# A recurrence and an MLP on one core: the seven-product form for one more token group, and two score buffers in every unit

## The chip, the cores and the metric

The kernel runs on one core of a Trainium2 chip. A core has TensorE (PE, matrix products), VectorE (DVE), ScalarE (ACT), GpSimd (POOL) and SyncE (SP), each with a queue of its own that it works off in order, and DMA engines that all of them can start. The metric is the device time of one execution in microseconds, as the median over several runs.

## The reference

A gated linear recurrence with complex decays over 768 steps for 4 x 8 heads of width 48, and behind it an MLP with squared ReLU over all 3072 tokens, all of it in float32:

```python
mag = np.sqrt(a_re * a_re + a_im * a_im)
scale = np.minimum(mag, 0.999) / (mag + 1e-06)
a_re_n, a_im_n = (a_re * scale, a_im * scale)
for t in range(S):
    ar, ai = (a_re_n[:, :, t, :, None], a_im_n[:, :, t, :, None])
    new_re = ar * S_re - ai * S_im
    new_im = ar * S_im + ai * S_re
    kv = np.einsum('bhd,bhe->bhde', k[:, :, t], v[:, :, t])
    S_re, S_im = (new_re + kv, new_im)
    y[:, :, t] = np.einsum('bhd,bhde->bhe', q[:, :, t], S_re)
x = y.transpose(0, 2, 1, 3).reshape(3072, 384)
h = x @ w_in            # 384 x 2048
out = np.maximum(h, 0.0) ** 2 @ w_out   # 2048 x 384
```

## The kernel before

**Units.** The 3072 tokens are cut into six units of 512. For each unit the kernel does a *chain*, then *pairs*, then *dense*. The chain (VectorE and ScalarE above all) makes the decays' running products and from them two scaled arrays, Q~ and K~. `pairs` takes the heads in four pairs: Q~ and K~ are turned (the tokens into the columns) into a buffer `QT`; TensorE makes the scores of two heads (`sc`), VectorE multiplies them by a causal mask into a buffer `A`, and a mix of A with the values v and of Q~ with the running state gives the outputs (`yp`), which are copied and moved by DMA into `xT`. In all units but the first, the turning is four transposes on VectorE, copies on ScalarE and nine DMAs, eight of them from SyncE's queue. `dense` is the MLP, in two groups of 256 tokens: a hidden layer of 48 matmuls of 256 columns into three PSUM blocks d0 to d2, ReLU and square on ScalarE into `g`, and a second layer.

**The second layer in three forms.** The plain form (the end of `dense`) multiplies each of the two 128-token halves by all 16 blocks of w_out: 2 x 16 matmuls of 384 columns. `eight` cuts tokens, hidden width and output width in two each and makes eight products. `seven` does the same with seven products, by sums and differences of operands: each product is two calls of `half` with four matmuls of 192 columns, so 56 matmuls. It needs sums of quarters of w_out, made once by `sums_of_w2` on VectorE (eight instructions, which also overwrite a quarter of w_out in place, so that the plain form can't be used afterwards), sums of quarters of g for each group (`put`, eight on VectorE), and seven additions of 128x192 into the output tiles (`add`).

**Who uses which.** Groups are named (unit, group). The list `SEVEN` has the groups in the seven-product form: both groups of the units 1 to 5. Unit 0 has the plain form in both.

**Shared space.** A tile `T` of 4608 columns has three thirds. While the weights are brought in it stages raw pieces of them; in unit 1 it is a third QT buffer, a third A buffer and the second value buffer `vv[1]`; from `sums_of_w2` on it holds the three sums of quarters of w_out. `ROOM` is the number of units, counted from the first, that use this: `vs(n)` gives the value buffer, and unit 1 has three QT and three A buffers, where all others have two.

**What sets the order.** The program is a list of steps with their reads and writes. A planner (`Plan.order`) puts them into a sequence for each engine: of the steps that are ready at the time, the one with the lowest number in the table `ORDER` goes first. Where it counts on a longer stop of TensorE it puts in small matmuls of the identity (`idle`). The sequence is fixed when the kernel is built; on the chip an instruction starts when all ahead of it in its engine's queue have, and its data are there.

**Lines.** L1850 is the hidden layer's matmul, L1897 the plain second layer's, L2051 a `half` of the seven-product form, L2065 a `put`, L2074 an `add`, L2036 the sums of w_out, L1679 a transpose of `turn` and L1691 its DMAs, L1732 the scores, L1738 the mask, L1762 the new state (`keep`), L1777 its sums on VectorE, L1790 and L1794 the mix, L880 the identity matmuls, L1076 the loads of decays, Q and K, and L1091 those of v. L1143, L1153, L1214, L1228, L1243, L1247, L1248, L1265, L1270 and L1277 are the chain's products on VectorE.

Of the kernel before, what the change touches and what calls it, by code (L numbers as in the profile page):

```python
# [767 lines left out]
def fast_path(ctx, tc, q, k, v, a_re, a_im, moe_w_in, moe_w_out, out, flag, ots, blocks_of):  # L768
# [1073 lines left out]
    def dense(n, grp):  # L1842
# [43 lines left out]
        if n >= FAST:  # L1886
            (seven if joint else eight)(n, grp)
            return
# [380 lines left out]
```

## Time and profile before

| | us |
|---|---|
| median of three runs | 650.94 (650.93 to 651.6) |
| the profiled execution | 652.71 |
| its span | 651.0 |
| granted TensorE clock in it, mean | 0.997 |
| first dense matmul of unit 0 | 84.84 |
| first scores of unit 1 | 151.20 |
| first dense matmul of unit 1 | 186.28 |
| first dense matmul of unit 2 | 283.50 |

The profile is of one execution. It gives every instruction's start and length by engine, what ended the idle time before it, and the landing of DMAs; times within it are from the span's start. A float32 matmul leaves two records, and the recorded lengths of neighbours overlap, so that the pace of TensorE is read from the length of a row of matmuls and not from the mean of one. Lines are those of the kernel before; in the kernel after, lines behind the table are one higher, and two less than that between the removed and the added call of `sums_of_w2`.

### The profile page before, as it was taken

Reading aid. Unit: us, or ns where it says so; the run is one execution under the profiler, and the core shown is the slowest. Engines: PE = TensorE matmul, PEld = TensorE weight load, DVE = VectorE, ACT = ScalarE, POOL = GpSimd, SP = SyncE. Lnnn points to the kernel's source line nnn. Section 1 sums busy time; section 2 is a strip of 40 time slices with the busy share of each in tenths; the row PEclk is TensorE's granted clock in tenths of the full one; section 3 lists DMA queues with packets and bytes.
Section 4 is the critical chain, followed back from the end, with each engine's and each line's share of the span. In section 5 each row is a group of like instructions: output and inputs, shape, how many; then the busy total and the mean of one; then the engine's idle time right before and its main releaser. Section 6 shows DMA issues by size and latency. Waiting matters only on the chain.

```text
span 651.0 us, 13374 instructions
## 1 busy us (share of the span) xinstructions
PE 641.1 (98%) x5046; PEld 575.9 (88%) x5046; DVE 571.2 (88%) x1187; ACT 382.8 (59%) x652; POOL 152.4 (23%) x258
## 2 busy tenths in 40 slices
PE   8998999999999999999999999999999999999998
PEld 7988987578778988999988998989999989988997
DVE  7999999999799998988997996995979998359993
ACT  7989889956665265368166648156658164145500
POOL 6503455123200022051043051121050030022210
PEclk9998999999999999999999999999999999999999
DMA  7972679237620156352176354165260162257651
GB/s 224 298 255 57 163 213 203 72 89 189 165 82 2 37 126 149 93 143 52 49 161 146 73 131 88 24 152 159 58 171 16 45 143 66 61 202 242 209 184 31
DMA packets 34630, 81.79 MB, mean 126 GB/s; under 512 B 7894, under 2 KB 13411, under 8 KB 34556
## 3 DMA queue, kind: packets, MB, share of 16 engines
q0 software_dynamic: 17024, 58.60, 33.6%
q1 hardware_dynamic: 15356, 20.04, 12.1%
q10 hardware_dynamic: 2176, 2.20, 1.2%
q8 instruction: 42, 0.69, 0.5%
q14 instruction: 32, 0.26, 0.1%
HBM read 48.76 MB, written 4.72 MB: 82 GB/s over the span
## 4 chain that ended last, share of the span: by engine, by line
PE 73%; DVE 12%; ACT 4%; DMA 3%; issue 2%; SPq 0%; POOL 0%; DVEq 0%; ACTq 0%; POOLq 0%
PE d L1850 24%; PE d L2051 24%; PE d L1897 5%; PE sc L1732 5%; PE yp L1790 3%; PE tr L1762 2%; PE d L1943 2%; PE yp L1794 2%; PE tr L1943 2%; DVE f L1243 1%; PE sc L1943 1%; DMA aq<-in_a_im_dram 1%; PE d L1710 1%; DVE g L2065 1%; DVE aq L1228 1%
## 5 line engine op out<-in xcount | busy, mean ns | idle before, releaser
L1850 PE MATMUL d<-xT,w 128*128 128x256 f32 x912 | 203.2, 380 | 0.0
L1850 PEld LDWEIGHTS d<-xT,w 128*128 128x128 f32 x912 | 171.8, 190 | 24.0 <-issue 0.4
L2051 PE MATMUL d<-w,g 128*128 128x192 f32 x576 | 101.0, 327 | 0.0
L2051 PEld LDWEIGHTS d<-w,g 128*128 128x128 f32 x576 | 94.3, 190 | 1.2 <-issue 0.4
L1882 ACT ACTIVATE g<-d 128x512 f32<-128x512 f32 x76 | 45.0, 592 | 81.7 <-PE d L1850 79.0
L2051 PE MATMUL d<-T,g 128*128 128x192 f32 x432 | 77.1, 329 | 0.4 <-DVE g L2065 0.3
L2051 PEld LDWEIGHTS d<-T,g 128*128 128x128 f32 x432 | 70.6, 190 | 2.0 <-DVE g L2065 0.6
L2007 POOL DMA_DIRECT2D out_dram<-ot x22 | 12.5, 569 | 202.3 <-DVE ot L2074 181.3
L1682 ACT COPY QT<-aq 32x512 f32<-32x512 f32 x57 | 35.0, 615 | 39.7 <-DVE aq L1679 27.9
L1639 POOL DMA_DIRECT2D KC<-f x56 | 35.0, 630 | 80.8 <-DVE f L1593 30.3
L2065 DVE TENSOR_TENSOR g<-g 128x512 f32<-128x512 f32 x72 | 48.1, 685 | 4.8 <-PE d L2051 4.0
L1883 ACT ACTIVATE g<-g 128x512 f32<-128x512 f32 x80 | 50.5, 631 | 2.6
L1679 DVE STREAM_TRANSPOSE aq<-f 128x768 f32<-128x768 f32 x40 | 49.0, 1277 | 0.3
L1800 ACT COPY yt<-yp 112x512 f32<-112x512 f32 x24 | 26.5, 1106 | 34.2 <-PE yp L1794 34.2
L880 PEld LDWEIGHTS d<-ident 128*128 128x128 f32 x348 | 42.6, 203 | 3.0 <-POOL ident masks.py:199 1.7
L880 PE MATMUL d<-ident 128*128 128x128 f32 x348 | 43.3, 287 | 1.7 <-POOL ident masks.py:199 1.7
L1593 DVE TENSOR_TENSOR f<-aq 128x768 f32<-128x768 f32 (+1 forms) x56 | 44.0, 838 | 0.5
L1897 PE MATMUL d<-w,g 128*128 128x384 f32 x128 | 43.7, 491 | 0.0
L1732 PE MATMUL sc<-QT 96*64 96x128 f32 (+1 forms) x736 | 41.0, 258 | 1.5 <-ACT QT L1713 0.8
L1732 PEld LDWEIGHTS sc<-QT 96*64 96x64 f32 x736 | 37.1, 140 | 4.6 <-issue 2.3
L1738 DVE TENSOR_TENSOR A<-sc,mask 128x512 f32<-128x512 f32 x45 | 29.8, 681 | 9.2 <-PE sc L1732 9.2
L1897 PEld LDWEIGHTS d<-w,g 128*128 128x128 f32 x128 | 23.7, 190 | 15.0 <-issue 0.4
(276 smaller groups left out, 1167.5 us busy)
## 6 DMA issues: line engine op xcount, KB each, us to landing
QT<-aq SPq DMA_DIRECT2D x152, 64.0 KB
f<-in_moe_w_in_dram POOLq DMA_DIRECT2D x8, 768.0 KB, 6.0
f<-in_moe_w_out_dram POOLq DMA_DIRECT2D x8, 768.0 KB, 5.0
out_dram<-ot POOLq DMA_DIRECT2D x22, 192.0 KB, 2.8
KC<-f POOLq DMA_DIRECT2D x20, 192.0 KB, 4.5
xT<-yt SPq DMA_DIRECT2D x36, 96.0 KB
aq<-in_q_dram POOLq DMA_DIRECT2D x8, 384.0 KB, 5.4
aq<-in_k_dram POOLq DMA_DIRECT2D x8, 384.0 KB, 5.7
```

What stands on the lines that cost most here:

```text
L880: plan = Plan(lambda b: pe.matmul(bank[b][:, 0:C], lhsT=ident, rhs=ident, start=True, stop=True), ["d2", "d1", "d0"], lambda ap: tc.nc.val ...
L1593: lambda j=j, r=r, o=o: dve.tensor_tensor(out=o[:, :, :, r * D:(r + 1) * D], in0=qk[:, j], in1=a[:, r], op=ALU.mult), late[z])
L1639: lambda i=i, queue=queue, lo=lo, hi=hi, a0=a0, a1=a1: queue.dma_start(out=kc[lo:hi, i], in_=nat[a0:a1]),
L1679: lambda nat=nat, dst=dst, j=j: dve.transpose(out=dst[:, j], in_=nat), rank)
L1682: lambda b=b, t=t, T6=T6: act.copy(out=t[32 * b:32 * b + 32, b], in_=T6[32 * b:32 * b + 32, i % 2, b]),
L1732: pe.matmul(sa[r:r + C // 2, j, :, lo:32], lhsT=T[:, j, 1, h, ts(late, C // 2)], rhs=T[:, j, 0, h].rearrange("p (c t) -> p c t", c=W)[:, : ...
L1850: pe.matmul(ps, lhsT=w1[:, f // FP, m, ts(f % FP, C)], rhs=xT[:, n % 2, m, ts(grp, G)], start=(m == 0), stop=(m == NM - 1))
L1882: act.activation(out=o, in_=ps, func=AF.Relu)
L1883: act.activation(out=o, in_=o, func=AF.Square)
L1897: pe.matmul(ps, lhsT=gt[:, f % 2, ts(i, C)], rhs=w2[:, f], start=(f == 0), stop=(f == NF - 1))
L2051: pe.matmul(bank[b][:, 0:DH], lhsT=gs(r, h)[:, j - 4 * h], rhs=w(j), start=first and j == 0, stop=last and j == NT - 1)
L2065: step("DVE", tt(4 * C), gk(x0, h) + gk(x1, h), gk(o, h), lambda: dve.tensor_tensor(out=gs(o, h), in0=gs(x0, h), in1=gs(x1, h), op=op), (0 ...
```

## The change

1. `SEVEN` is now all groups but the very first, so (0,1), the second group of the first unit, takes the seven-product form too. Its hidden layer is made in the pairs of blocks that this form needs (`fs`).
2. `sums_of_w2` is called behind the dense step of (0,0) instead of behind the pairs of unit 1. As it overwrites part of w_out, it must come behind the last plain product, which is now one group earlier, and its results go into the tile T.
3. T is then no longer free in unit 1, so `ROOM` goes from 2 to 1: unit 1 has two buffers of Q~ and of scores, as all others, and its values go into the first value buffer, in which unit 0 had its own.
4. The table `ORDER` has other numbers throughout.

```diff
-    ROOM = max(FAST, 2)
-    SEVEN = [(n, grp) for n in range(FAST, NU) for grp in range(2)]
+    ROOM = 1
+    SEVEN = [(n, grp) for n in range(NU) for grp in range(2)][FAST:]
...
-        fs = [(j, j + NT) if n >= FAST else (2 * j, 2 * j + 1) for j in range(NT)]
+        fs = [(j, j + NT) if joint else (2 * j, 2 * j + 1) for j in range(NT)]
...
-        if n >= FAST:
-            (seven if joint else eight)(n, grp)
+        if joint:
+            seven(n, grp)
             return
...
-        if n == FAST:
-            sums_of_w2()
...
                 dense(n, grp)
+            if (n, grp + 1) == SEVEN[0]:
+                sums_of_w2()
```

How the instructions stand now, at three places. The first is TensorE's queue ahead of the first scores of unit 1 (w1 and w2 are w_in and w_out, g the hidden layer, sc the scores, KC the gathered K~). Before:

```order
L1897 MATMUL d2_66<-w2_75,g_100 128x384 x2
L1850 MATMUL d1_65<-xT_99,w1_74 128x256 x6
L1850 MATMUL d2_66<-xT_99,w1_74 128x256 x6
L1850 MATMUL d1_65<-xT_99,w1_74 128x256 x6
L1850 MATMUL d0_64<-xT_99,w1_74 128x256 x6
L1897 MATMUL d1_65<-w2_75,g_100 128x384 x8
L1850 MATMUL d0_64<-xT_99,w1_74 128x256 x6
L1850 MATMUL d2_66<-xT_99,w1_74 128x256 x6
L1732 MATMUL sc1_114<-QT1_82 64x128 x8
```

After:

```order
L1898 MATMUL d2_66<-w2_75,g_100 128x384 x6
L1851 MATMUL d0_64<-xT_99,w1_74 128x256 x6
L1851 MATMUL d2_66<-xT_99,w1_74 128x256 x6
L1851 MATMUL d0_64<-xT_99,w1_74 128x256 x6
L1851 MATMUL d2_66<-xT_99,w1_74 128x256 x6
L1851 MATMUL d1_65<-xT_99,w1_74 128x256 x3
L881 MATMUL d0_64<-ident_101 128x128 x3
L1851 MATMUL d2_66<-xT_99,w1_74 128x256 x6
L1851 MATMUL d1_65<-xT_99,w1_74 128x256 x6
L1763 MATMUL tr1_116<-v0_85,KC0_83 64x48
```

The eight output matmuls of the second group that stood there are gone, and three identity matmuls stand there (two more stand earlier, ahead of the turning of the chain's totals). From the first dense matmul of unit 0 up to here the queue has 90 hidden-layer matmuls in both, and 40 output matmuls before against 32 now; the half products of the second group all stand behind this point.

The second place is VectorE's queue in the pairs of unit 1, up to its last two masks (St and S are the running state, g the operand sums' tile, f and aq the chain of unit 2). Before:

```order
L1738 TENSOR_TENSOR A0_93<-sc0_113,mask_103 128x512
L1265 SCALAR_TENSOR_TENSOR f0_78<-f0_78 128x4x144
L1228 TENSOR_TENSOR aq0_76<-aq0_76,f0_78 128x1536
L1270 TENSOR_TENSOR f0_78<-f0_78 128x4x48
L1243 TENSOR_TENSOR f0_78<-aq0_76 128x768 x2
L2036 TENSOR_TENSOR w2_75<-w2_75 128x4x192
L1777 TENSOR_TENSOR St1_96<-tr0_115,S1_92 96x96
L1777 TENSOR_TENSOR S0_91<-tr0_115,St1_96 96x96
L1143 TENSOR_TENSOR f1_79<-f1_79 128x768
L1738 TENSOR_TENSOR A0_93<-sc1_114,mask_103 128x512
L1738 TENSOR_TENSOR T_80<-sc0_113,mask_103 128x512
```

After:

```order
L2075 TENSOR_TENSOR ot0_62<-ot1_63,d2_66 128x192
L1374 TENSOR_REDUCE sums_104<-xn_90 128x1
L1154 SCALAR_TENSOR_TENSOR f0_78<-f0_78 128x768
L1158 SCALAR_TENSOR_TENSOR f0_78<-f0_78 128x768
L1144 TENSOR_TENSOR f1_79<-f1_79 128x768
L1215 SCALAR_TENSOR_TENSOR f0_78<-f0_78 128x768
L1229 TENSOR_TENSOR aq0_76<-aq0_76,f0_78 128x1536
L1244 TENSOR_TENSOR f0_78<-aq0_76 128x768 x2
L1778 TENSOR_TENSOR St1_96<-tr0_115,S1_92 96x96
L1778 TENSOR_TENSOR S0_91<-tr0_115,St1_96 96x96
L1739 TENSOR_TENSOR A0_93<-sc0_113,mask_103 128x512
L1739 TENSOR_TENSOR A1_94<-sc1_114,mask_103 128x512
```

Counted from the program's start to the last mask of unit 1, VectorE's queue has eight more operand sums (L2065), six more sums of w_out (L2036) and two more additions (L2074), and one L1265 and one L1270 fewer. Before the first mask of unit 1 the two queues hold the same work but for one L1373, and before the first transpose of unit 1 but for one L1277, which now stand behind.

The third place is SyncE's queue in the same pairs (yt are the outputs on their way to xT). Before:

```order
L1691 DMA QT1_82<-aq0_76 32x512 x8
L1691 DMA T_80<-aq0_76 32x512 x8
L1691 DMA QT0_81<-aq1_77 32x512 x8
L1691 DMA QT1_82<-aq1_77 32x512 x6
L1808 DMA xT_99<-yt0_97 48x512
```

After:

```order
L1692 DMA QT0_81<-aq0_76 32x512 x8
L1692 DMA QT1_82<-aq0_76 32x512 x8
L1692 DMA QT0_81<-aq1_77 32x512 x8
L1809 DMA xT_99<-yt0_97 48x512 x2
L1692 DMA QT1_82<-aq1_77 32x512 x8
```

The third pair's copies go into the first pair's buffer now, so they have to wait until the first pair's mix has read it, and the fourth pair's for the second pair's mix.

261 rows, old and new, of the table ORDER are left out of this document.

## The prediction

> **What bounds the kernel now.** First the page: busy shares, then the forty slices.
>
> ```profile
> span 651.0 us, 13374 instructions
> PE 641.1 (98%) x5046; PEld 575.9 (88%) x5046; DVE 571.2 (88%) x1187; ACT 382.8 (59%) x652; POOL 152.4 (23%) x258
> ...
> PE   8998999999999999999999999999999999999998
> DVE  7999999999799998988997996995979998359993
> ```
>
> TensorE is busy in every slice, so whatever leaves its queue should shorten the run. But VectorE is at 9 too, from the second slice to about the thirteenth (16 us each), and only later falls to 5 to 8. The change lies in that first part, so the share alone doesn't say which engine sets the pace there. I therefore cut the part into three stages at events of TensorE (the view of windows; columns: length, busy time and instructions of PE, weight loads, DVE, ACT, POOL, granted clock, DMA share, GB/s).
>
> ```profile
> 85.00:151.20 66.20, 66.20 (x273) 50.20 (x273) 64.52 (x132) 54.74 (x90) 23.70 (x36) 1.00 0.60 142
> 151.20:186.28 35.08, 34.72 (x397) 26.14 (x397) 29.75 (x45) 25.22 (x41) 9.02 (x13) 1.00 0.67 177
> 186.28:283.50 97.22, 96.65 (x781) 89.10 (x780) 90.32 (x185) 50.35 (x87) 10.79 (x18) 1.00 0.29 76
> ```
>
> Stage A (85.0 to 151.2) is the first unit's dense work on TensorE, beside the second unit's chain on VectorE; both are full. Stage B (151.2 to 186.28) is the second unit's head pairs, with what is left of the first unit's dense work as filler. Stage C is the second unit's dense work up to the third unit's. Why does B begin at 151.2? The timeline, rows of four engines:
>
> ```profile
> 139.60 3.28 DVE L1679 STREAM_TRANSPOSE aq<-f 128x768 f32<-128x768 f32 x3
> 142.23 6.42 SPq L1691 DMA_DIRECT2D QT<-aq  x8
> 151.01 0.77 POOL L1076 DMA_DIRECT2D aq<-in_a_im_dram  x1 [8.51 <-DMA T<-aq]
> 151.20 1.09 PE L1732 MATMUL sc<-QT 96*64 96x128 f32 x16
> ```
>
> VectorE turns the first pair, SyncE issues eight copies of it until 148.65, and GpSimd, whose next load overwrites their source, is let go at 151.01. The first scores follow at 151.20. So B starts when VectorE's data arrive, and TensorE's queue ahead of it happened to be just long enough. That is the row on which my forecast turns.
>
> **The change, part by part.**
>
> *Products.* In the chain of waits:
>
> ```profile
> 111.66 9.03 PE d L1897 x28
> ...
> 613.69 26.00 PE d L2051 x160
> ```
>
> One matmul is two records. A 384-column one takes 2 x 9.03/28 = 0.645 us, a 192-column one 2 x 26.00/160 = 0.325 us. The old group has 32 of the first, 20.6 us; the new one 14 half products of 4, 56 of the second, 18.2 us. TensorE saves 2.4 us. ScalarE has one narrow copy for two wide ones and is busy 25.22 of 35.08 us in B: nothing.
>
> *Stage A.* The order ahead of the second unit's first scores keeps 90 hidden-layer matmuls but loses 8 of the group's 32 output matmuls, 8 x 0.645 = 5.2 us (the new products all stand behind those scores). The scores cannot come 5.2 us sooner: VectorE's queue ahead of the first pair's transposes is the same but for one L1277, which costs about 0.7 us. So B starts near 150.5, and TensorE idles for about 4.5 us in A, partly under the five identity matmuls now put there.
>
> *Stage B, TensorE alone.* It is busy 34.72 us. Out go 24 output matmuls (15.5 us), in come the 18.2 us: 37.4 us. From 150.5 that ends at 187.9 instead of 186.28. So with no further wait the saving has already become a loss of 1.6 us.
>
> *Stage B, VectorE.* It gets eight operand sums (L2065), most of the weight sums (L2036; they used to lie partly in C) and adds (L2074):
>
> ```profile
> L2065 DVE TENSOR_TENSOR g<-g 128x512 f32<-128x512 f32 x72 | 48.1, 685 | 4.8 <-PE d L2051 4.0
> L2074 DVE TENSOR_TENSOR ot<-ot,d 128x192 f32<-128x192 f32 x70 | 23.8, 349 | 13.8 <-PE d L2051 9.8 <-issue 3.5
> L1265 DVE SCALAR_TENSOR_TENSOR f<-f 128x576 f32<-128x576 f32 x12 | 8.9, 750 | 0.9 <-ACT f L1222 0.9
> L1270 DVE TENSOR_TENSOR f<-f 128x192 f32<-128x192 f32 x24 | 8.1, 352 | 0.3
> L2036 DVE TENSOR_TENSOR T<-w 128x768 f32<-128x768 f32 x4 | 3.8, 952 | 0.1
> ```
>
> In a row such instructions start sooner than their durations say:
>
> ```profile
> 179.14 0.68 DVE L1738 TENSOR_TENSOR A<-sc,mask 128x512 f32<-128x512 f32 x1
> 179.74 0.68 DVE L1738 TENSOR_TENSOR T<-sc,mask 128x512 f32<-128x512 f32 x1
> ...
> 196.97 0.96 DVE L2036 TENSOR_TENSOR T<-w 128x768 f32<-128x768 f32 x1
> 197.84 0.95 DVE L2036 TENSOR_TENSOR T<-w,T 128x768 f32<-128x768 f32 x1
> ```
>
> That is 0.60 and 0.87 us, 0.08 less than they last. Up to the last mask of the second unit, VectorE's queue gains 8 x 0.60, 6 x 0.87 and 2 x 0.26, and loses one L1265 (0.67) and one L1270 (0.27): 9.6 us more. Against this stand its waits in B before that mask:
>
> ```profile
> 161.62 0.69 DVE L1738 TENSOR_TENSOR T<-sc,mask 128x512 f32<-128x512 f32 x1 [1.17 <-PE sc L1732]
> 162.57 0.25 DVE L1777 TENSOR_TENSOR St<-tr,S 96x96 f32<-96x96 f32 x1 [0.26 <-ACT St L1770]
> 165.16 0.96 DVE L1153 SCALAR_TENSOR_TENSOR f<-f 128x768 f32<-128x768 f32 x1 [1.50 <-ACT f L1150]
> 168.81 0.69 DVE L1738 TENSOR_TENSOR A<-sc,mask 128x512 f32<-128x512 f32 x1 [0.83 <-PE sc L1732]
> 177.94 0.25 DVE L1777 TENSOR_TENSOR St<-tr,S 96x96 f32<-96x96 f32 x1 [1.43 <-ACT St L1770]
> ```
>
> 5.2 us that more work can fill. The last mask ended at 179.74 + 0.68 = 180.4, so it now ends at 180.4 - 0.7 + 9.6 = 189.3 less what is filled, 184.1 at best. Behind it come the mix and two half products:
>
> ```profile
> 181.99 0.39 PE L1794 MATMUL yp<-QT,St 96*48 96x128 f32 x4
> 182.31 4.14 PE L1897 MATMUL d<-w,g 128*128 128x384 f32 x12
> 186.28 9.23 PE L1850 MATMUL d<-xT,w 128*128 128x256 f32 x42
> ```
>
> From the mask's end to the end of the mix is 182.3 - 180.4 = 1.9 us, two half products are 8 x 0.325 = 2.6. Dense work of unit two thus begins at 188.6 if all 5.2 us are filled (2.3 late) and at 193.8 if none are (7.5 late). I take 3.7 us filled, hence 190.1, **3.8 us late**. I leave 1.5 us open because of the buffers.
>
> *Two buffers for three.* The third pair's turned data must now wait for the first pair's mix. Before, the decays of the unit after were loaded late for such a reason already:
>
> ```profile
> 168.38 0.75 POOL L1076 DMA_DIRECT2D aq<-in_a_re_dram  x1 [7.09 <-DMA QT<-aq]
> ```
>
> That load waits for the third pair's copies, which now wait longer, and VectorE's queue has the work on it just ahead of the last two masks. Cost between 0 (the wait is covered by the 9.6 us of other work; a buffer less brings nothing sooner) and 5.2 (new waits as long as all the old ones). I take the 1.5 that I left open above, nearer to the lower end, since most of that other work stands ahead of this point in the queue.
>
> *Value buffer, loads.* Unit two's values move to unit one's buffer, free after the mixes of unit one at about 85; the row at 139.60 shows them unneeded for 55 us more. Nothing.
>
> *Stage C and on.* VectorE ends its next chain with 8 sums and 7 adds more than before, 8 x 0.60 + 7 x 0.26 = 6.6 us, less the 3.7 filled: about 3 us late. TensorE, 3.8 late itself, needs that unit at
>
> ```profile
> 283.50 6.85 PE L1850 MATMUL d<-xT,w 128*128 128x256 f32 x31
> ```
>
> plus 3.8, so nothing is added. Behind 283.5 nothing is changed in kind, and 3.8 us stay to the end. The span is 651.0, its execution 652.71, the median 650.94; I add to the median: **654.7**.
>
> *A rule weighed.* The trace has a cooled array:
>
> ```profile
> 52.00:57.00 5.00, 4.11 (x37) 1.00 0.12 20
> 57.00:62.00 5.00, 4.18 (x37) 0.66 0.52 102
> ...
> 58.46 3.60 PE sc L1732 x32
> ...
> 75.19 1.34 PE sc L1732 x32
> ```
>
> (Windows of PE alone, the fourth number being the clock; then two rows of the chain.) After pauses of about 0.9 us around 57 the clock fell to 0.66, and 32 score records took 3.60 us, not 1.34: 2.3 us lost. The Trainium skill, "TensorE: Matmul & The Clock Gate", section "What's actually happening", has the clock halved after an idle window of some 3.4 us; by it 4.5 us of idle time in one piece would cool the array and the pieces would not. Here short pauses were enough once, so the trace is harsher than the Trainium skill. The sum goes without a cooled array: five identity matmuls stand in the gap, and stages B and C show 1.00 with 0.36 and 0.57 us of idle time.
>
> **The rivals.**
>
> 1. *VectorE's additions hide* (18%). B is then TensorE's own 37.4 us, and C swallows its 97.22 - 96.65 = 0.57 us of idle time: 1.6 - 0.6, so 652.0. For it: 5.2 us of waits to fill. Against: the masks stand in the same queue, behind 9.6 us more.
> 2. *Stage A isn't VectorE's* (10%). If the turned data could be there by 146.0, TensorE would never pause and the 2.4 us come through: 648.5, faster. It decides at 5.2 us sooner. For it: weight pieces reach VectorE earlier, as the third value buffer no longer shares their space. Against: A has only 66.20 - 64.52 = 1.7 us of VectorE time to win.
> 3. *Nothing is filled* (10%). The two buffers make new waits as long as those that go: 7.5 late, 658.4. For it: the load row at 168.38.
> 4. *The array cools* (10%). The pause ahead of the scores costs 2.3 us on top: 3.8 + 2.3, so 657.0.
>
> **How the numbers follow.** The forecast, with 1.5 us more or 2.1 less filled, has 52%: 653.2 to 656.8. With rivals 3 and 4, slower has 72%; rival 1 lies within 0.2% (1.3 us, about what can be told from no change), 18%; rival 2 gives 10% to faster. The range 650.3 to 658.0 leaves out rival 2 and most of rival 3.
>
> **What would show it.** Right: TensorE idle, or on identity matmuls, for 4 to 5 us between 100 and 151; first scores of unit two at 150 to 151; its last mask ending at 184 to 188; L1851 of unit two from about 190; no new pause later. Wrong: first scores before 148 (rival 2), dense work of unit two from 188 (rival 1), a clock under 1.00 in stage A (rival 4), or a gap at the third unit's start, which would mean that VectorE's lag outlasts TensorE's.

## The result, and the profile after

The kernel after takes 655.72 us (median of 10 runs, 654.47 to 656.59), the kernel before, run beside it, 651.05 (10 runs). The ratio is 1.0059, with a 95% interval from 1.0033 to 1.0085: slower by 2.1 to 5.5 us. The forecast was 654.7, in a range from 650.3 to 658.0, and slower. So sign, size and range hold. Whether the reasons hold is another question, and the larger part of what follows says that one of them doesn't, and that the size came out partly by luck.

The page of the profile after (an execution of 655.2 us), its busy shares and VectorE's slices:

```profile
span 653.4 us, 13567 instructions
PE 642.8 (98%) x5132; PEld 584.6 (89%) x5132; DVE 579.1 (89%) x1202; ACT 381.9 (58%) x651; POOL 151.3 (23%) x258
...
DVE  7999999999999999988998997995979999459993
PEclk9999999999999999999999999999999999999999
```

The 7 in VectorE's eleventh slice (163 to 179 us) is gone: it is now at 9 from the second slice to the seventeenth. The same three stages in the view of windows, as cut for the prediction (length, then busy time of PE, weight loads, DVE, ACT, POOL, granted clock, DMA share, GB/s):

```profile
85.00:150.55 65.55, 64.85 (x286) 50.56 (x285) 64.09 (x131) 52.73 (x85) 18.14 (x29) 1.00 0.50 126
150.55:189.72 39.17, 38.33 (x462) 35.62 (x462) 38.20 (x59) 24.77 (x42) 9.15 (x13) 1.00 0.59 159
189.72:287.24 97.52, 96.91 (x781) 89.00 (x781) 89.82 (x187) 52.88 (x92) 15.26 (x24) 1.00 0.33 84
```

Stage B, the pairs of unit 1 (called the second unit in places of the prediction), is 39.17 us long and was 35.08. VectorE is busy in 38.20 of it and was in 29.75; TensorE in 38.33, where it was in 34.72. By this view either engine may be the bound. TensorE's timeline at the turns:

```profile
84.81 2.50 PE L881 MATMUL d<-ident 128*128 128x128 f32 x20
87.14 0.60 PE L1851 MATMUL tr<-xT,w 128*128 128x256 f32 x2
...
143.99 0.83 PE L881 MATMUL d<-ident 128*128 128x128 f32 x6
...
150.55 0.90 PE L1763 MATMUL tr<-v,KC 128*64 128x48 f32 x24
151.37 2.07 PE L1733 MATMUL sc<-QT 96*64 96x128 f32 x32
...
179.78 0.89 PE L1733 MATMUL sc<-QT 96*64 96x128 f32 x16
182.65 0.91 PE L1733 MATMUL sc<-QT 96*64 96x128 f32 x16
...
189.72 9.23 PE L1851 MATMUL d<-xT,w 128*128 128x256 f32 x42
...
287.24 9.23 PE L1851 MATMUL d<-xT,w 128*128 128x256 f32 x42
```

The reader is to see four things. Twenty identity records (ten matmuls) stand ahead of unit 0's dense work, which begins at 87.14 and not at 84.84. The pairs of unit 1 begin at 150.55, with the matmuls of the new state; their first scores follow at 151.37, a little behind the 150 to 151 that the prediction named. Their fourth pair has its scores at 179.78 and 182.65. Dense work of unit 1 begins at 189.72, 3.44 us later than in the profile before, that of unit 2 at 287.24, 3.74 later. VectorE's last masks of unit 1:

```profile
184.01 1.27 DVE L1739 TENSOR_TENSOR A<-sc,mask 128x512 f32<-128x512 f32 x2
```

They end at 185.28, inside the 184 to 188 that the prediction named, and 190.1 was named for 189.72. From these rows alone the prediction's story looks confirmed.

### The profile page after: what moved, and what is told of

It is laid out like the page before. It is cut to its first block, busy times and chain, and to the rows that moved or that the text cites. A ratio compares the mean times of both kernels' runs of the same rounds, so it can differ in the third digit from the quotient of the medians.

```text
span 653.4 us, 13567 instructions
## 1 busy us (share of the span) xinstructions
PE 642.8 (98%) x5132; PEld 584.6 (89%) x5132; DVE 579.1 (89%) x1202; ACT 381.9 (58%) x651; POOL 151.3 (23%) x258
## 4 chain that ended last, share of the span: by engine, by line
PE 67%; DVE 21%; ACT 5%; DMA 3%; issue 2%; POOL 2%; SPq 0%; ACTq 0%; DVEq 0%; POOLq 0%
PE d L2052 27%; PE d L1851 19%; PE sc L1733 4%; PE d L881 3%; PE yp L1791 3%; PE d L1944 2%; PE yp L1795 2%; PE tr L1763 2%; DVE w L982 2%; DVE f L1594 2%; PE tr L1944 2%; DVE f L1244 1%; DMA aq<-in_k_dram 1%; PE sc L1944 1%; DVE A L1739 1%
## 5 line engine op out<-in xcount | busy, mean ns | idle before, releaser
L2052 PE MATMUL d<-w,g 128*128 128x192 f32 x640 | 112.3, 327 | 0.0
L2052 PEld LDWEIGHTS d<-w,g 128*128 128x128 f32 x640 | 104.9, 190 | 1.6 <-issue 0.6
L2052 PE MATMUL d<-T,g 128*128 128x192 f32 x480 | 86.6, 329 | 0.5 <-DVE g L2066 0.5
L2052 PEld LDWEIGHTS d<-T,g 128*128 128x128 f32 x480 | 78.5, 190 | 2.6 <-DVE g L2066 1.1
L2066 DVE TENSOR_TENSOR g<-g 128x512 f32<-128x512 f32 x80 | 53.3, 686 | 10.8 <-PE d L2052 5.7
L881 PEld LDWEIGHTS d<-ident 128*128 128x128 f32 x386 | 47.3, 202 | 3.2 <-POOL ident masks.py:199 1.7
L881 PE MATMUL d<-ident 128*128 128x128 f32 x386 | 48.4, 286 | 1.7 <-POOL ident masks.py:199 1.7
L1683 ACT COPY QT<-aq 32x512 f32<-32x512 f32 x60 | 36.9, 616 | 15.7 <-PE yp L1795 9.7
L2075 DVE TENSOR_TENSOR ot<-ot,d 128x192 f32<-128x192 f32 x77 | 26.0, 349 | 14.0 <-PE d L2052 10.1
L1791 PE MATMUL yp<-A,v 128*48 128x128 f32 x384 | 36.9, 276 | 0.5 <-DVE A L1739 0.5
```

The costliest lines, as they stand in the source:

```text
L881: plan = Plan(lambda b: pe.matmul(bank[b][:, 0:C], lhsT=ident, rhs=ident, start=True, stop=True), ["d2", "d1", "d0"], lambda ap: tc.nc.val ...
L1683: lambda b=b, t=t, T6=T6: act.copy(out=t[32 * b:32 * b + 32, b], in_=T6[32 * b:32 * b + 32, i % 2, b]),
L1791: pe.matmul(ypair[64 * h:64 * h + D, ts(j, C)], lhsT=v5[:, j, 2 * i + h], rhs=aa[h][:, j], start=True, stop=at[j] is None)
L2052: pe.matmul(bank[b][:, 0:DH], lhsT=gs(r, h)[:, j - 4 * h], rhs=w(j), start=first and j == 0, stop=last and j == NT - 1)
L2066: step("DVE", tt(4 * C), gk(x0, h) + gk(x1, h), gk(o, h), lambda: dve.tensor_tensor(out=gs(o, h), in0=gs(x0, h), in1=gs(x1, h), op=op), (0 ...
```

## The experiments

Theory V is the prediction's: VectorE sets where the pairs begin, and its 9.6 us of added work in them makes most of the loss, the buffers 1.5 us. Theory K: the third buffer of Q~ makes it. Theory T: TensorE's own work in the pairs makes it. Where a kernel has other waits than before or after, its table `ORDER` was set anew by a search over the kernel's own planner, which is less thorough than the one behind the two kernels at hand; so a loss in such a run may be partly one of its order. In such a table's kernel the lines may stand lower: by 14 in the first two and by 13 to 14 in the last, where L1718 and L1719 are the scores, L1836 and L1837 the hidden layer and L866 the identity matmuls. In the kernel without identity matmuls they stand two higher.

### The buffers alone

```diff
-    ROOM = max(FAST, 2)
+    ROOM = 1
```

> The kernel before with ROOM = 1 alone: the second unit (unit 1) has two buffers of Q~ and scores and the first value buffer; the plain form and the sums of w_out stay where they were, and the table of numbers is set anew for this program. Theory V (VectorE's longer queue in the pairs of unit 1 makes the loss, the buffers at most 1.5 us of it): 651.0 to 652.6 us, dense work of unit 1 starts at 186.3 to 187.8 in the trace. Theory K (the buffers make nearly all of the loss, because the third and fourth pair have to wait for the mixes of the first and second): 654 to 656 us, dense work of unit 1 from 189 or later, although VectorE has none of the additions. Theory T (TensorE's own work in the pairs of unit 1, grown by what no longer fits ahead of them, makes the loss): as V.

655.77 us (6 runs), ratio 1.0075 (1.0058 to 1.0092): as slow as the whole change, and K's number. The product form and the operand sums are those of the kernel before. The sums of w_out are not quite: the call stands where it stood, but the tile T is free sooner, and the order for this kernel has all eight of them ahead of the last masks of unit 1, seven of them in the pairs (6.4 us of VectorE), where the kernel before has two. So the run sets the operand sums aside, but not the sums of w_out. Four rows of its TensorE timeline, then one of SyncE's queue and one of VectorE:

```profile
168.78 1.51 PE L1718 MATMUL sc<-QT 96*64 96x128 f32 x32
177.45 0.83 PE L866 MATMUL d<-ident 128*128 128x128 f32 x6
180.42 1.57 PE L1718 MATMUL sc<-QT 96*64 96x128 f32 x32
185.32 0.43 PE L1776 MATMUL yp<-A,v 128*48 128x128 f32 x4 [1.80 <-DVE A L1724]
```

```profile
168.99 7.14 SPq L1677 DMA_DIRECT2D QT<-aq  x8
...
183.90 1.28 DVE L1724 TENSOR_TENSOR A<-sc,mask 128x512 f32<-128x512 f32 x2
```

The second pair's mix ends at 168.8, and only then may the eight copies of the fourth pair start, into the buffer that this mix has read. SyncE issues them from 168.99 to 176.13. The scores come at 180.42, the masks end at 185.2 behind work of the next chain that stood ahead of them in VectorE's queue, and the last mix starts at 185.32. That is a chain of 16.5 us from one mix to the other, and TensorE has not enough other work for it: it runs 28 identity records and stands for 1.80 us.

The same wait stands in the kernel after. First what SyncE's queue waited for a mix between 140 and 192 us, in the kernel after and then in the kernel before (us in total, times, the longest); then five rows of the chain of waits in the kernel after:

```profile
SPq L1692 <- PE yp L1795: 5.1, 2, 3.0
...
SPq L1691 <- PE yp L1794: 0.2, 1, 0.2
```

```profile
169.60 0.24 PE yp L1795 x4
169.84 0.02 issue
169.86 0.52 SPq L1692
...
170.48 1.86 DMA QT<-aq
172.34 0.84 ACT f L1146
```

The second pair's mix ends at 169.84, a copy of the fourth pair follows at once, and when it has landed ScalarE goes on with a step of the next chain (f). VectorE's products of that chain stand ahead of the last masks. Ahead of the mix the same chain of waits runs through VectorE's new sums, so both causes have a part in it. In all profiles of this study with two buffers of Q~ the total of this wait is 1.7 to 6.7 us, in all with three at most 0.4.

The windows of its pairs add a warning:

```profile
148.89:188.22 39.33, 37.53 (x426) 29.48 (x425) 38.06 (x56) 24.97 (x40) 10.41 (x16) 1.00 0.62 163
```

VectorE is busy in 38.06 of 39.33 us here too, with none of the operand sums. When the pairs take longer it does other work in the meantime, of the next chain and the seven sums of w_out. Its full row in the kernel after was no proof that it set the pace.

### Seven products, three buffers

```diff
-    ROOM = 1
+    ROOM = 2
...
-    def w_t(r):
-        return lambda j: TW[:, r, j]
+    def w_t(r, n, h):
+        if n < FAST:
+            return w_lo(0), parts_of(h, 0)
+        return (lambda j: TW[:, r, j]), [("T", r, h)]
```

(with the three calls of `half` that use it changed to match, and `sums_of_w2` where it stood before.)

> The kernel after with ROOM = 2: the second group of unit 0 in seven products, but three buffers of Q~ and scores in unit 1. As the space of the sums of w_out is then taken, these sums are made behind the pairs of unit 1 as in the kernel before, and the six half products of that one group that need them read w_out itself (so the output of 256 tokens isn't the reference's). The table of numbers is set anew. Theory V: VectorE keeps eight operand sums and two additions more in the pairs, 5.3 us against 5.2 us of waits, and the gap in the stage before stays: 652 to 653.5 us. Theory T: the gap stays and TensorE's rows of half products stay: 652.5 to 654 us. Theory K: the loss goes with the buffers: 649 to 651.5 us, dense work of unit 1 from 187 or earlier.

651.76 us (12 runs), ratio 1.0006 (0.9989 to 1.0023). It lies a quarter of a microsecond above K's range and below those of V and T. The chain is short again:

```profile
175.52 1.46 PE L1719 MATMUL sc<-QT 96*64 96x128 f32 x30
...
186.59 5.78 PE L1837 MATMUL d<-xT,w 128*128 128x256 f32 x23
```

With the buffer the seven products cost nothing that can be measured; without it the old form costs as much as the new one. Here too the buffer does not change alone: one sum of w_out stands ahead of the last masks, where the kernel after has eight.

### VectorE's additions left out

```diff
-            lambda: dve.tensor_tensor(out=gs(o, h), ...)       # put
+            lambda: n and dve.tensor_tensor(out=gs(o, h), ...)
...
-                     dve.tensor_tensor(out=o, in0=x0, in1=x1, op=ALU.subtract),   # sums_of_w2
+                     None,
```

> The kernel after without the eight operand sums (L2066) of the second group of unit 0 and without the eight sums of w_out (L2037), which leaves the products of seven undone as to their values; all else stands in the same order. VectorE has 8 x 0.60 + 8 x 0.87 = 11.8 us less in the pairs of unit 1. Theory V: the pairs' stage falls from 39.2 to 37.4 us or less, TensorE's own time, and the run to 653.5 us or less. Theories T and K: TensorE was busy 38.33 of 39.17 us there, so the stage gains 0.8 us at most: 654.8 to 655.7 us.

653.74 us (6 runs), ratio 1.0049 (1.0031 to 1.0066). The interval overlaps that of the kernel after; the medians differ by 2.0 us, the starts of unit 1's dense work by 1.2. The window of the pairs and the row behind it:

```profile
150.40:188.56 38.16, 37.69 (x462) 35.48 (x462) 27.66 (x44) 24.93 (x42) 9.12 (x13) 1.00 0.60 163
```

```profile
188.56 9.23 PE L1851 MATMUL d<-xT,w 128*128 128x256 f32 x42
```

VectorE has 10.5 us less to do in the stage, and the stage is 1.0 us shorter. V wanted 37.4 us or less in the stage and 653.5 or less in the run, K and T 0.8 less at most and 654.8 or more; the stage is nearer to the latter, the run nearer to the former. So the additions are a part of the loss, 1 to 2 us by the profile and the medians, though the overlapping intervals don't establish it, and with all of them gone the run is still 0.3% to 0.7% slower than the kernel before. TensorE is busy in 37.69 of the 38.16 us: in this form its own work nearly fills the stage, and this run alone can't tell K from T.

### More work on VectorE ahead of the pairs

Four products of unit 1's chain are issued twice:

```diff
-                         lambda j=j, r=r, o=o: dve.tensor_tensor(...)
+                         lambda j=j, r=r, o=o: [dve.tensor_tensor(...)
+                             for _ in range(1 + ((n, z, p) == (1, 0, 0)))]
```

> The kernel after with four products of unit 1's chain (L1594, the last ahead of the turning of its first pairs) issued twice with the same result: 3.5 us more on VectorE ahead of the first scores of unit 1. If VectorE alone sets when unit 1's pairs begin (my step for the stage before the pairs): first scores 3.5 us later, at 154.7 to 155.2, TensorE idle longer by as much, and the run 3.0 to 3.8 us longer, 658.5 to 659.5 us. If transfers, SyncE's copies or TensorE set it (the rival): first scores at most 1.5 us later and the run within 1.5 us of the kernel after.

659.49 us (4 runs), ratio 1.0137 (1.0114 to 1.0160), 3.8 us above the kernel after: VectorE sets where the pairs begin. The first scores were later than expected, though, at 156.69:

```profile
146.07 1.65 PE L881 MATMUL d<-ident 128*128 128x128 f32 x6 [2.39 <-ACT g L1883]
148.61 7.53 PE L1851 MATMUL d<-xT,w 128*128 128x256 f32 x24 [0.89 <-ACT g L1883]
```

```profile
135.00:156.00 21.00, 17.72 (x71) 14.65 (x69) 20.70 (x28) 11.22 (x20) 2.96 (x5) 0.84 0.36 79
```

The longer pauses, 2.39 and 0.89 us, brought the clock down to 0.84 (the window's clock, third number from the end), and 24 records took 7.53 us where 5.45 were needed in the kernel after. The pairs took back 1.6 us of it.

### Which of the three things of `ROOM`

`ROOM` sets three things: a third buffer of Q~, a third of scores, and a second value buffer. First two buffers of Q~ alone in the kernel before, then two of scores alone, then three of Q~ without the other two:

```diff
-            s = take("QT", 3 if 0 < n < ROOM else 2)
+            s = take("QT", 2)                        # first kernel
...
-            a = take("A", 3 if 0 < n < ROOM else 2)
+            a = take("A", 2)                         # second and third
...
-        return n % 2 if n < ROOM else 0
+        return 0                                     # third
```

> The kernel before with two buffers of Q~ in unit 1 instead of three, and nothing else: three buffers of scores, the second value buffer, the plain form and the sums of w_out stay as they were; the table of numbers is set anew for this program. If the third buffer of Q~ is what the change pays for (theory K, narrowed): 654 to 656 us, as with ROOM = 1 (655.77), and the fourth pair's scores at 179 or later, against 176.3 before. If the buffer of scores or the value buffer is it: 650.5 to 652.5 us.

664.48 us (6 runs, 659.72 to 669.12), ratio 1.0199 (1.0153 to 1.0245), far above what any theory had. The order found for it stalls at other places, too:

```profile
133.69 14.51 PE L1850 MATMUL d<-xT,w 128*128 128x256 f32 x66 [1.24 <-ACT ot L1902]
...
196.23 0.77 PE L1305 MATMUL tr<-perm,xn 128*128 128x128 f32 x5 [2.22 <-DVE xn L1248]
```

The second of these pauses belongs to the next chain and has nothing to do with the buffer. The direction agrees with K; the size of the run says nothing. Its pairs can be read, however: they begin at 153.30, dense work of unit 1 at 191.15, so that they take 37.9 us where the kernel before needs 35.1, with one sum of w_out in them and with 20 identity records on TensorE.

> The kernel before with two buffers of scores (A) in unit 1 instead of three, and nothing else, in the same table of numbers. If the third buffer of Q~ is the cause: no change, 650.5 to 652.0 us. If the masks' buffers are it: 653 to 656 us.

650.98 us (12 runs), ratio 1.0003 (0.9983 to 1.0023): nothing hangs on the buffer of scores.

> The kernel before with the other two of the three things that ROOM = 1 changes and without the first: unit 1 has three buffers of Q~, but two of scores and the first value buffer; plain form and sums of w_out as before, table of numbers set anew. With ROOM = 1 whole it was 655.77 us. If the third buffer of Q~ is what costs: 650.5 to 652.5 us, the fourth pair's scores near 176 as before. If the value buffer costs (the values of unit 2 can then be loaded only behind unit 1's mixes, not 100 us ahead): 653.5 to 656 us, and the loss shows behind unit 1's dense work has begun.

649.67 us (12 runs), ratio 0.9978 (0.9961 to 0.9995): nothing hangs on the value buffer either, and the loss of the first experiment is gone with the third buffer of Q~ back (and with the sums of w_out late again, one of them ahead of the last masks). Its copies and its fourth pair:

```profile
154.37 9.14 SPq L1691 DMA_DIRECT2D QT<-aq  x12
...
165.56 2.56 SPq L1691 DMA_DIRECT2D QT<-aq  x4
```

```profile
173.10 0.89 PE L1732 MATMUL sc<-QT 96*64 96x128 f32 x16
...
183.96 3.40 PE L1850 MATMUL d<-xT,w 128*128 128x256 f32 x15
```

SyncE has issued the fourth pair's copies at 168.1, 8 us sooner than with two buffers, and the scores come at 173.10 where they came at 180.42.

### The kernel before once more, and with a warm array

> The kernel before, unchanged, for a second profile: the one at hand is of an execution of 652.71 us, 1.7 above the median. If that excess lies behind the stages of the change, the starts of the pairs and of the dense work of unit 1 come out within 0.3 us of 151.2 and 186.3 and those of the units behind come sooner; if it lies ahead of them or in them, these starts move by 0.5 us or more.

This execution took 654.11 us. Unit 0's dense work began at 84.80, the scores of unit 1 at 151.2, dense work of unit 1 at 187.33: as slow as in the first profile from the start, and 1 us slower in the pairs. Both profiles have the clock at 0.66 at 57 to 62 us. The run with two buffers of scores, whose instructions stand in the same order, has the same pauses there and no cooled array; its dense work of unit 0 begins at 83.25, its scores of unit 1 at 149.69, its dense work of unit 1 at 184.75, and its span is 648.2. So the profile on which the forecast was worked out is some 1.5 us late from 60 us on, and the kernel after, whose order has identity matmuls at that place, is not. To see whether the pauses do it:

```diff
-            many, b = self.fill.get(n, (0, None))
+            many, b = {219: (3, "yp"), 223: (4, "yp")}.get(n) or self.fill.get(n, (0, None))
```

> The kernel before with seven identity matmuls more: three and four in the two pauses of 0.8 to 0.9 us at 56 to 58 us, ahead of unit 0's first scores, where the clock fell to 0.66 in both of its profiles. If that cooled array is the 1.5 us by which those executions lie above the median: dense work of unit 0 from 83.5 or sooner instead of 84.8, no run with a mean clock under 0.998, median 649.5 to 650.7 us. If the clock falls there for another reason: as before, 651.2 us with single runs at 653 to 655.

649.68 us (12 runs), ratio 0.9979 (0.9960 to 0.9998). No run had a mean clock under 0.999. Windows of this kernel, then of the second profile of the kernel before:

```profile
52.00:57.00 5.00, 4.76 (x43) 4.57 (x43) 4.99 (x19) 5.00 (x9) 1.63 (x3) 1.00 0.24 37
57.00:62.00 5.00, 5.00 (x82) 4.47 (x80) 5.00 (x16) 4.97 (x5) 1.57 (x3) 1.00 0.47 98
```

```profile
52.00:57.00 5.00, 4.09 (x38) 3.84 (x36) 4.99 (x18) 5.00 (x8) 1.54 (x3) 1.00 0.12 20
57.00:62.00 5.00, 4.20 (x37) 3.62 (x37) 5.00 (x16) 4.97 (x6) 1.66 (x4) 0.66 0.52 103
```

Filling the pauses keeps the clock up in this profile, dense work of unit 0 begins at 83.36, and the kernel is faster than both kernels of this study, if only by 0.02% to 0.4% than the one before. The cooled array is not all of that: of the 61 runs of the kernel before that stand beside these experiments, ten have a mean clock under 0.999 and a median of 654.3 us, but the 51 others have one of 651.2. What else the seven matmuls changed stays open.

### Identity matmuls taken out, banks, and late sums

```diff
             many, b = self.fill.get(n, (0, None))
+            if 80 < self.start[n] < 152:
+                many = 0
```

> The kernel after without the 30 identity records that stand in TensorE's queue between 84 and 145 us (20, 4 and 6), so that TensorE is idle there instead. If the array cools in such a pause (my rival 4, 2.3 us by the rows of the kernel before): granted clock under 1.00 at 85 to 100 us and 656.5 to 658.5 us. If pauses of 0.8 to 2.5 us don't cool it: 655 to 656.5 us with the clock at 1.00. VectorE sets when this stage ends, so the dense work of unit 0 may start up to 2.3 us sooner with no gain.

656.28 us (6 runs), ratio 1.0077 (1.0049 to 1.0104), no gain and no cooled array there:

```profile
87.27 0.67 PE L1853 MATMUL tr<-xT,w 128*128 128x256 f32 x2 [1.83 <-DMA xT<-yt]
```

```profile
85.00:90.00 5.00, 3.17 (x15) 2.48 (x15) 4.95 (x6) 4.72 (x6) 1.28 (x3) 1.00 0.26 61
```

Where the twenty identity records stood, TensorE now waits for the last outputs of unit 0, to within 0.2 us of where those records ended.

```diff
+            if (n, grp) == (0, 1) and f2 > 4:
+                b = ("sc0", "sc1", "yp")[f2 - 5]
...
```

> The kernel after with the last three pairs of hidden blocks of the second group of unit 0 made in two banks of the scores and that of the outputs, which frees the three banks of the dense work sooner, and the table of numbers set anew. By its order VectorE turns unit 1's first pair some 2 us sooner. If nothing of the stage ahead of the pairs can come sooner (my step): first scores at 150.5 or later and 655 to 656.5 us. If VectorE's order there leaves room (a weaker form of the rival that this stage isn't VectorE's): first scores at 148 to 149 and 653.3 to 654.8 us, still above the kernel before.

656.51 us (10 runs, 653.35 to 671.78), ratio 1.0074 (1.0041 to 1.0107). The first scores do come at 147.87 in its profile, with the same work on VectorE as in the kernel after, and dense work of unit 1 at 187.52; but the profiled execution, 653.35 us, is the fastest of its runs, and the median shows no gain. So with another order, and three blocks in other banks, the first scores can come 3.5 us sooner; which of the two does it wasn't separated. Dense work of unit 1 comes only 2.2 us sooner: the pairs take 39.7 us. Why the other runs are slower wasn't settled.

The last kernel keeps the third buffer of Q~ and the seven products by making two of the three sums of w_out only when that buffer is free (its other edits are left out here):

```diff
+                    (b01, b01, b00, [], lo), (t4, b11, b01, lo + up, 2), (t4, b10, t4, up, 2),
+                    (t2, b11, b01, lo + up, 1), (t3, t2, b00, lo + [("T", 1, h)], 0)):
```

> A form of the change that keeps the third buffer of Q~ in unit 1: two buffers of scores and the first value buffer as after, but the two sums of w_out whose space that buffer needs are made late, from the second pair's mix on, and in another order (ten instructions on VectorE instead of eight); the second group of unit 0 is in seven products, and its products that need those sums come last. Table of numbers set anew; nothing is left out. If the third buffer of Q~ is what the change pays for: 652 to 654 us, 2 to 3.5 us faster than the kernel after, not faster than before. If VectorE's additions are: 655 us or more, since there are two more of them.

657.43 us (6 runs), ratio 1.0091 (1.0063 to 1.0120): a miss for K as written. Its profile has a stall ahead of the pairs that its order made, in ScalarE's queue, and a cooled array behind it:

```profile
121.88 5.49 PE L1837 MATMUL d<-xT,w 128*128 128x256 f32 x12 [3.33 <-ACT g L1869]
```

```profile
120.00:125.00 5.00, 3.12 (x7) 2.50 (x8) 4.55 (x22) 4.91 (x13) 0.00 (x0) 0.59 0.02 6
```

Twelve records took 5.49 us there, not 2.75. The stage ahead of the pairs is spoilt by that, and whether the idea would pay with a better order stays open. The pairs themselves are short: they begin at 159.24 and dense work of unit 1 at 193.64, 34.4 us, although fifteen of the sums stand in them ahead of the last masks.

## Why the prediction held, and where its reasons did not

The two buffers and the two forms make a table of four, in us:

| | plain form in (0,1) | seven products in (0,1) |
|---|---|---|
| three buffers of Q~ | 651.2 (before) | 651.76 |
| two buffers of Q~ | 655.77 | 655.72 (after) |

The loss goes with the third buffer, in either form. The seven products neither gain nor cost anything that the medians show. But the two rows of the table differ in one thing more: with two buffers the orders have all eight sums of w_out ahead of the last masks of unit 1, with three buffers one or two. So the table by itself does not say whether the wait for a free buffer or VectorE's sums make the loss. The lengths of the pairs do, from one profile each (sums: those of w_out and of g that stand in the pairs ahead of the last masks; pairs and dense work of unit 1, in us):

| kernel | buffers of Q~ | sums | pairs from | dense work from | between |
|---|---|---|---|---|---|
| before | 3 | 2 | 151.20 | 186.28 | 35.1 |
| three of Q~ without the other two | 3 | 1 | 150.89 | 183.96 | 33.1 |
| seven products, three buffers | 3 | 8 | 151.94 | 186.59 | 34.7 |
| late sums | 3 | 15 | 159.24 | 193.64 | 34.4 |
| two of Q~ alone | 2 | 1 | 153.30 | 191.15 | 37.9 |
| additions left out | 2 | 0 | 150.39 | 188.56 | 38.2 |
| buffers alone | 2 | 7 | 148.89 | 188.22 | 39.3 |
| after | 2 | 16 | 150.55 | 189.72 | 39.2 |

The six other profiles lie in the same two bands, 34.4 to 36.2 with three buffers and 37.5 to 39.7 with two. Without the third buffer the pairs take some 3 us more even where one sum or none stands in them; with it fifteen sums do not lengthen them. The sums add about 1 us where the buffer is missing. Nor do TensorE's new products make the length: two of the kernels with two buffers have the plain form and put identity matmuls into the time. What stays open is how much of the 3 us TensorE's own work would keep in the kernel after if it had the buffer, for the two kernels with the products and three buffers make a part of these products outside the pairs.

- *Products.* A long row runs as the term said. Short rows don't: by the view of groups over stage B the 112 half-product records took 11.3 + 8.9 = 20.2 us, where the sum had 18.2, and the 48 output records that left took 17.0, where it had 15.5. Net 0.5 us more, a part of why TensorE was busy for 38.33 us and not for 37.4.
- *Stage A.* Right in its mechanism: VectorE sets its end (3.5 us more on it cost 3.8), the pairs begin at 150.55 where 150.5 was forecast, and TensorE has 4.7 us to spare, 3.9 on identity matmuls and 0.8 idle by the view of groups over the stage. Wrong in the place: about half of the gap, 85.0 to 87.14, lies ahead of unit 0's dense work, and behind 100 us there are 2.0 us of it, where the prediction's sign was 4 to 5. The 150.5 was met because the profile before is late: against an undisturbed one (149.69) the pairs begin 0.9 us later, not 0.7 sooner. And "the scores cannot come 5.2 us sooner" was not put to the test in full, but another order had them 3.5 us sooner, at 147.87.
- *Stage B, VectorE.* Times right, cause wrong. The last masks and the start of dense work came within 0.4 us of the forecast, but leaving out 11.8 us of additions moved that start by 1.2 us only. The step took an engine that fills up for the engine that sets the pace. That the time still came out is luck: the 2.3 us that the sum gave to VectorE's queue are too much by about 1, and the 1.5 for the buffers are too little by as much or more.
- *Two buffers for three.* This is the step that failed: "Cost between 0 ... and 5.2 ... I take the 1.5". In the length of the pairs it is some 3 us. By the ratios of the first experiment and of the one with three buffers of Q~, 1.0075 and 0.9978, it is 1.0%, 6.3 us, and by the nearer ends of their intervals 4.1, but that takes in the sums of w_out and whatever else the two orders differ in; against the kernel before itself it is 4.5. The range was made of VectorE's waits in the profile before. The price is made of something else: a pair's copies hold SyncE for 7 us, then land, then come scores, masks and mix, and with two buffers this chain can't begin before the mix two pairs earlier is done. That the copies of the third and the fourth pair have to wait for a mix was known when the change was described; the prediction read it for what it delays on GpSimd.
- *Value buffer, loads.* "Nothing" was right. The buffers of scores, for which the sum has no term, don't matter either.
- *Stage C and on.* Right, if like is set beside like: 3.44 us late became 3.74 at unit 2, but by the same two profiles only 2.4 in the span. Against the profile without a cooled array (the next point) it is 5.0 at unit 1, 5.5 at unit 2 and 5.2 in the span: nothing was swallowed.
- *The profile and the median.* The profile before was of an execution with a cooled array, so that its rows lie 1.5 us late (not the 2.3 of the prediction: the same 32 score records took 1.97 us in the other profile, against 3.60). Against the profile without it (an execution of 649.96 us, 1.0 under its kernel's median) the kernel after is 5.0 us late at unit 1's dense work and 5.2 in its span. The forecast added a difference from the cooled profile to a median of runs of which most had a warm array, and came out 1.0 us low.
- *The rivals.* Rival 3, the two buffers as long new waits, came nearest to the cause, and had 10%. Rival 4, a cooled array in stage A, did not happen, nor without the identity matmuls. Rival 2 holds in part, as above, but without its gain. Rival 1 is half right: the additions hide for the most part, though not the loss.
- *The rule weighed.* The Trainium skill, "TensorE: Matmul & The Clock Gate", section "What's actually happening", has the clock fall after an idle window of about 3.4 us. The pause of 3.33 us in the last experiment is near that length and agrees (0.59), and so does that of 1.83 us that left it at 1.00. The pauses of 0.8 and 0.9 us at 57 us do not: the clock fell in two of three profiles of the same order. The Trainium skill, "TensorE: Matmul & The Clock Gate", section "A second HAM failure mode: psum-queue depth-cycling", tells of another kernel in which frequent short pauses lower the clock; the two pauses here point the same way.

## What to carry to other kernels

An edit that takes a buffer away is to be priced by the chain that the buffer cut: from the use that frees it, through the copies that refill it and their queue, to the use behind, and then by what the bound engine has to do in that time; VectorE's waits in the profile before said nothing of it here. An engine that becomes busy throughout a stretch may just be doing later work early: take its added work out, and see whether the stretch gets shorter. Where the order of the instructions is made anew for an experiment, look in the queues for what else has moved. And compare profiles of the same clock, since a cooled array early in one of them moves every later row.

## What was not expected of the hardware

Pauses of 0.8 and 0.9 us, one behind the other, with TensorE busy in 4.1 of 5 us, went with a granted clock of 0.66 in two profiles of three, and a pause of 2.39 with one of 0.89 with 0.84; a single pause of 1.83 us with 3.17 busy of 5 left it at 1.00, and so did one of 1.02 us with 3.93 busy of 5 in the kernel after. With seven small matmuls in the first two of these pauses the kernel before was 0.2% faster (0.02% to 0.4%).
